# First two batches' strided attention in 32-query form, probabilities turned in place, and the second weight's columns permuted, in an attention and gated-feed-forward kernel

## The chip, the cores and the metric

The kernel runs on one core of a Trainium2 chip. The metric is the device time in microseconds (us) of one launch. The engines are named as the profile names them: PE (TensorE matmul) and PEld (its weight load), DVE (VectorE), ACT (ScalarE), POOL (GpSimd) and SP (SyncE, which issues nearly all DMAs).

## The reference

Eight batches of eight heads (576 positions, 64 wide) go through masked attention: heads 0 to 3 see the last 32 positions ("local"), heads 4 to 7 see earlier positions with the same remainder modulo 32 ("strided"). The result, 4608 rows of 512, goes through a feed-forward layer.

```python
scores = scale * np.matmul(q, k.transpose(0, 1, 3, 2))
mask_local = (rel >= 0) & (rel < stride)                     # stride = 32
mask_strided = (rel >= 0) & (pos[None, :] % stride == pos[:, None] % stride)
scores = np.where(masks[None, :, :, :], scores, -1000000000.0)
attn = np.exp(scores - np.max(scores, axis=-1, keepdims=True))
attn = attn / (np.sum(attn, axis=-1, keepdims=True) + 1e-09)
attn_out = np.matmul(attn, v).astype(np.float32)
x = attn_out.transpose(0, 2, 1, 3).reshape(B * S, H * D)
h = x @ w_in                                                 # 512 -> 2048
g = h * np.clip(h + 3.0, 0.0, 6.0) / 6.0
return g @ w_out                                             # 2048 -> 512
```

## The kernel before

**Work.** Heads go in pairs (`pair(g)`): in a batch the pairs 0 and 1 are local, 2 and 3 strided. A pair is loaded, turned so that the 64 features lie on partitions (for batch 0 by matmuls with an identity, L364; later by DVE), multiplied to scores (L593 or L601), put through the softmax on DVE, POOL and ACT, turned again, and multiplied with the values (L381, L392 or L728). The output of a pair is one 128-row piece of x, one of four along the 512 features. `keep_x` (L402) puts it away. In batches 0 and 1 each piece is split at once in a high part (ACT, L419) and the remainder (DVE, L422), since the feed-forward's matmuls take each fp32 number as two parts and multiply three times (high by high, high by low, low by high).

**Feed-forward.** Batches 0 to 2 run plainly (`ffn`, L807): L848 to L850 make a 128-column chunk of h from the four pieces of x and the first weight `wi`, ACT, DVE and POOL gate and split it, L825 to L827 multiply it with the second weight `wo`. Batches 3 and 4 run as one `super_tile` (L1165), and batches 5, 6, 7 and the last 64 rows of all batches in two `fast_tile` calls (L1263), with fewer products by Strassen's scheme. In `fast_tile` the gated values are the moving operand and pieces of the second weight the stationary one (L1441 to L1446): the 128 output columns of one product are taken with `w[:, q, h, d::2]`, every second column of 256.

**Weights.** They arrive as 8-byte numbers. `weight_part` (L258) loads 512 KB from SP, ACT makes the upper and lower bits (L281, L285), DVE joins them (L289), ACT or POOL makes the high part (L295, L297) and POOL the remainder (L301). There are 32 such loads, 16 of them issued in the first 37 us.

**Strided pairs.** With `wide` (batch 0 and batches 2 to 7) a strided pair has 32 score matmuls of 64 queries and 36 keys (L593); half of each result is of use, and four ACT copies for each head pick it (L619), after which POOL adds the mask (L633). Without it (batch 1) there are 64 matmuls of 32 queries and 18 keys (L601), and one DVE operation reads the scores and adds the mask (L626). An fp32 matmul of these kinds stands in the trace as two matmuls and two weight loads, so these are 64 and 128 in its counts. Probabilities are turned in batches 0 and 1 by DVE, block by block into the operand's tile (`turn`, L677 and L680; the very first pair by matmuls, `stand`, L364 with the name `pe`). From batch 2 on DVE turns them in place (`flip`, L683) and ACT sets the blocks out (`spread`, L690 and L693).

**Order.** The order of all instructions is set before the run by `Plan.emit` (L96): each step has an engine or a choice of engines, a cost, and a due time (`T0` is the time at which batch 0's feed-forward is wanted). A list scheduler walks through its own clock and writes the instructions in that order; each engine then runs its own stream in order, and waits at an instruction for what it needs. Where the planner sees PE idle by over 0.64 us in the first 100 us, it writes matmuls without use there (`idle`, L1550; L1560 is the first group, L1562 the later ones).

Of the kernel before, what the change touches and what calls it, by code (L numbers as in the profile page):

```python
# [29 lines left out]
TOK = 512  # L30
TURNS = ((0, 2, 1, 3), (2, 0, 3, 1)) + ((0, 2, 1, 3),) * 6
AHEAD = 27.0
OPEN = 6.0
HIENG = {"ACT": 0.63, "POOL": 0.7}

T0 = 44.0
TILE = 98.5
SUPER = 182.0  # L40
SECOND = 142.0
# [132 lines left out]
def attention_ffn(ctx: ExitStack, tc, q, k, v, w_in, w_out, out):  # L174
# [85 lines left out]
    def weight_part(k, w, g, i):  # L260
        key = wkey(w, g, i)
        fc = FQ * g if w == "i" else FQ * g + i + 1
        due = T0 + fc * TILE / NFC - 5.0 + 0.01 * k
        fkey = ("x", 1, 1 - (k // 2 % 2 if k < 20 else 0), k % 2)
        name = f"{w}{g}{i}"

        def load():
            if w == "i":
                src = w_in[i * P:(i + 1) * P, g * TOK:(g + 1) * TOK]
            else:  # L270
                src = w_out[(g * FQ + i) * P:(g * FQ + i + 1) * P, :]
            raw = new(wp, key, [P, TOK, 2], I32, f"raw{name}")
            nc.sync.dma_start(raw, src.bitcast(I32).rearrange("p (n t) -> p n t", t=2))
# [12 lines left out]

        def join():
            f = tiles[fkey]
            nc.vector.scalar_tensor_tensor(out=f, in0=f, scalar=3, in1=bits(),  # L289
                                           op0=ALU.logical_shift_left, op1=ALU.bitwise_or)  # L290

        def hi(e):
            t = new(wp, key, [P, 2, TOK], F32R, f"w{name}")
            if e == "ACT":
                nc.scalar.copy(t[:, 0], tiles[fkey].bitcast(F32))  # L295
            else:
                nc.gpsimd.tensor_copy(t[:, 0], tiles[fkey].bitcast(F32))  # L297

        def lo():
            t = tiles[key]  # L300
            nc.gpsimd.tensor_tensor(out=t[:, 1], in0=tiles[fkey].bitcast(F32), in1=t[:, 0].bitcast(F32), op=ALU.subtract)  # L301
# [21 lines left out]
    def either(us):  # L323
        return {"POOL": us, "DVE": us}

    def zero(key, pool, shape, dtype, us, due, name):

        def go(e):
            on(e).memset(new(pool, key, shape, dtype, name), 0.0)
            if key[0] == "e":  # L330
                t = tiles[key]
                on(e).memset(t[:, :NQB * WIN].rearrange("p (u x) -> p u x", x=WIN)[:, :, 2 * PAD:], 1.0e-9)
                on(e).memset(t[:, NQB * WIN:NQB * WIN + 8 * PAD].rearrange("p (u x) -> p u x", x=PAD)[:, :, NPOS:NPOS + 1], 1.0e-9)
        op(either(us), 0, go, writes=[key], due=due)

    def timing(g):
        b = g // NPAIR
# [60 lines left out]
    def x_keys(b, c):  # L398
        return [("x", b, c, i) for i in range(2)] if b < 2 else [raw_key(b, c)]

    def keep_x(nm, b, c, puts, due):

        xk, lk = x_keys(b, c), ("left", c, b)
        strided = c >= NPAIR // 2
        begun = []
        for n, (bkey, what, place, size, rest) in enumerate(puts):
            def to(i, place=place, rest=rest):
                return place(left[c][:, LEFT * b:LEFT * b + LEFT] if rest else tiles[xk[i]])

            def homes():  # L410
                if not begun:
                    begun.append(1)
                    for i, x in enumerate(xk):
                        new(xp, x, [P, TOK], F32R if b < 2 else F32, f"x{nm}{i}")

            def hi(bkey=bkey, what=what, to=to, rest=rest):
                if not rest:
                    homes()
                nc.scalar.copy(to(0), what(tiles[bkey.key]))  # L419

            def lo(bkey=bkey, what=what, to=to):
                nc.vector.tensor_tensor(out=to(1), in0=what(tiles[bkey.key]), in1=to(0).bitcast(F32), op=ALU.subtract)  # L422
# [3 lines left out]
            op("ACT", 0.15 + size * (0.0019 if strided else 0.00085), hi, reads=[bkey] + (xk if rest else []), writes=kk, give=bkey if last and whole else None, due=due + n)  # L426
            if not whole:
                op("DVE", 0.15 + size * (0.002 if strided else 0.00105), lo, reads=[bkey], writes=kk, give=bkey if last else None, due=due + 0.2 + n)

# [3 lines left out]
    def pair(g):  # L433
# [237 lines left out]
        for j in range(2):  # L671
            def turn(j=j):
                at, e = tiles[akeys[j]], e_whole(j)
                for a in range(n // PAD):
# [3 lines left out]
                        continue  # L678
                    for h in range(2):
                        nc.vector.transpose(at[PAD * (a + h):PAD * (a + h) + PAD, :, rows], e[rows, :, PAD * h:PAD * h + PAD])  # L680
            if b >= 2:
                def flip(j=j):
                    nc.vector.transpose(e_whole(j)[:, :, :2 * PAD if loc else PAD], e_whole(j)[:, :, :2 * PAD if loc else PAD])  # L683

# [13 lines left out]
                op("ACT", 6 * 0.31 if loc else 4 * 0.36, spread, reads=[ekeys[j]], writes=[akeys[j]], due=due - 1.9 + j)  # L698
# [18 lines left out]
        def values():  # L717
# [12 lines left out]
        op("PE", 1.25 * slow, values, reads=[*akeys, *vkeys], writes=[*vb, *xk, lk], take=vb, due=due - 1001,  # L730
           room=0.0 if early else ROOM, mode="v")
        if first:
            half = S // 2
# [56 lines left out]

    def out_ops(i, uk, name, rows, due, last):
        def ob():
            o = new(xp, uk, [P, DM], F32, f"ob{name}_{i}")
            if last and i % 2:
                nc.vector.tensor_scalar_mul(o, tiles["acc", i], 1.0 / 6.0)
            else:
                nc.scalar.activation(o, tiles["acc", i], AF.Copy, scale=1.0 / 6.0)

        def store():
            o = tiles[uk]  # L800
# [9 lines left out]
    def ffn(b):  # L810
        s0, puts = start[b], []
        chunk = TILE / NFC
        xk = {c: x_keys(b, c) if b < 2 else [("x", 1, c, i) for i in range(2)] for c in range(NCC)}

        def mm2(fc, gk):
            wkeys = [wkey("o", fc // FQ, fc % FQ), wkey("o", fc // FQ, fc % FQ) + ("lo",)]
# [17 lines left out]
        def first_product(fc):  # L834
# [3 lines left out]
            for n_, c in enumerate(TURNS[b]):  # L838
                wkeys = [wkey("i", fc // FQ, c), wkey("i", fc // FQ, c) + ("lo",)]

                def mm1(n_=n_, c=c, wkeys=wkeys):
# [6 lines left out]
                    nc.tensor.matmul(ph, wih, xh, start=n_ == 0, stop=False)  # L848
                    nc.tensor.matmul(ph, wih, xl, start=False, stop=False)  # L849
                    nc.tensor.matmul(ph, wil, xh, start=False, stop=n_ == NCC - 1)  # L850
                op("PE", 0.683, mm1, reads=xk[c] + wkeys, writes=[pk],
                   due=s0 + (fc + n_ * 0.12) * chunk, mode="f")
            return fc, pk, uk, gk

# [430 lines left out]
    def fast_tile(si):  # L1285
# [87 lines left out]
        def second_of(s):  # L1373
# [5 lines left out]
            for j, nm in enumerate(SECONDS):  # L1379
# [53 lines left out]
                for d in range(2):  # L1433
                    bank = ("acc", d + 2 * (nm in ("P2", "P5", "P3")))

                    def mm(d=d, bank=bank, gks=gks, wk=wk, fresh=fresh, nm=nm):
# [3 lines left out]
                        w = home(wk).rearrange("p q (h d) -> p q h d", h=2)  # L1440
                        for q in range(2):  # L1441
                            gh, gl = (half_of(gks[q], x) for x in range(2))
                            wh, wl = (w[:, q, h, d::2] for h in range(2))
                            nc.tensor.matmul(acc, wh, gh, start=fresh and q == 0, stop=False, skip_group_check=not fresh)  # L1444
                            nc.tensor.matmul(acc, wh, gl, start=False, stop=False, skip_group_check=not fresh)  # L1445
                            nc.tensor.matmul(acc, wl, gh, start=False, stop=q == 1, skip_group_check=not fresh)  # L1446
# [62 lines left out]
    def first_tiles():  # L1509
        tiles["qplain"] = ap.tile([P, S + STRIDE * PAD], F32, tag="qq", name="qplain")  # L1510
        tiles["kplain"] = ap.tile([P, PAD + 2 * S], F32, tag="kk", name="kplain")
        nc.gpsimd.memset(tiles["kplain"][:, :PAD], 0.0)
        nc.gpsimd.memset(tiles["qplain"][:, S:].rearrange("c (r m) -> c r m", m=PAD)[:, :, NPOS:], 0.0)
        tiles["at64"] = ap.tile([P, 2, 3 * QB], F32, tag="vt", name="at64")
    op("POOL", 0.1, first_tiles, writes=["plain", ("at64", 0), ("at64", 1)], due=-30)
# [80 lines left out]
```

## Time and profile before

| what | before |
|---|---|
| runs, us | 873.19, 875.98, 877.65; median 875.98 |
| profiled execution: its time, its span | 873.75 us, 871.9 us |
| PE busy | 851.9 us (98%) |
| PEld, DVE, ACT, POOL busy | 687.7, 539.3, 557.8, 614.7 us |
| first matmul of the feed-forward (L848) | 38.96 us after the span's start |
| mean granted TensorE clock | 0.992 |
| moved by DMA | 179.12 MB, mean 205 GB/s |

The profiled time is 1.85 us longer than the span. Busy shares are means over the whole span: PE is busy nearly always, so a change matters where PE waits or where its matmuls take longer than they must. A row of the timeline gives the start, the length, the engine, the line and operation, the tiles, the shape and how many instructions were merged, and in brackets how long the engine sat idle before, and who ended that; "issue" stands for a wait for which the profile shows nobody. A row of the windows gives for each engine the busy time and, as (x...), the instructions in that stretch, then the granted TensorE clock as a share of the full one, the busy share of the 16 DMA engines, and GB/s.

### The profile page before, as it was taken

What the parts mean: (1) busy time and instruction counts of PE and PEld (TensorE: products, weight loads), DVE (VectorE), ACT (ScalarE), POOL (GpSimd) and SP (SyncE); (2) the same over time, 40 slices, a digit from 0 to 9 for tenths busy, and PEclk for the clock granted to TensorE, in tenths of its full rate; (3) what the DMA queues carried; (4) which work ended last, traced back from release to release, by engine and by line L of the source; (5) the groups of instructions that cost most, each with busy time, mean ns of one, the idle gap of its engine ahead of it and who ended that gap; (6) DMA issues with size and microseconds to landing.
All of it is one profiled execution on the core that took longest, in us unless ns stands there. A gap on an engine that the chain in (4) does not pass through costs nothing.

```text
span 871.9 us, 18946 instructions
## 1 busy us (share of the span) xinstructions
PE 851.9 (98%) x6962; PEld 687.7 (79%) x6962; DVE 539.3 (62%) x898; ACT 557.8 (64%) x1246; POOL 614.7 (70%) x606
## 2 busy tenths in 40 slices
PE   9889999999999999999999999999999999999996
PEld 6667778878878788888888888788888778888884
DVE  5698877344544548454546672566776987655586
ACT  3697657678778766777668855776645555454441
POOL 4688876688447799756767993666974978667572
PEclk9899999999999999999999999999999999999998
DMA  8968714888974456899999998976566577766536
GB/s 214 322 140 243 220 28 93 236 265 239 299 200 111 112 141 163 233 250 259 259 262 282 300 284 213 253 188 198 181 195 183 178 207 214 231 190 188 178 121 145
DMA packets 323308, 179.12 MB, mean 205 GB/s; under 512 B 182864, under 2 KB 300368, under 8 KB 323216
## 3 DMA queue, kind: packets, MB, share of 16 engines
q1 hardware_dynamic: 318564, 176.27, 71.9%
q10 hardware_dynamic: 4652, 1.64, 0.9%
q8 instruction: 55, 0.90, 0.4%
q14 instruction: 37, 0.30, 0.1%
HBM read 136.97 MB, written 40.89 MB: 204 GB/s over the span
## 4 chain that ended last, share of the span: by engine, by line
PE 87%; DMA 5%; POOL 3%; DVE 2%; issue 1%; ACT 1%; SPq 0%; ACTq 0%; POOLq 0%
PE P L1121 9%; PE P L1123 8%; PE P L1122 8%; PE cP L1444 6%; PE cP L1446 6%; PE cP L1445 6%; PE acc L825 5%; PE ph L848 5%; PE acc L827 5%; PE acc L826 4%; PE ph L850 4%; PE ph L849 4%; PE acc L1206 4%; PE acc L1208 3%; PE acc L1207 3%; PE pv L392 2%
## 5 line engine op out<-in xcount | busy, mean ns | idle before, releaser
L1462 DVE SCALAR_TENSOR_TENSOR C<-cP,C 128x512 f32<-128x512 f32 x96 | 65.7, 688 | 44.9 <-PE cP L1446 44.3
L787 POOL TENSOR_TENSOR gl<-u,gh 128x512 fp32r<-128x512 f32 x48 | 65.2, 1359 | 32.2 <-ACT gh L783 16.0
L1133 DVE TENSOR_TENSOR G<-P,G 128x512 f32<-128x512 f32 x64 | 44.0, 689 | 65.6 <-PE P L1123 52.8
L1121 PE MATMUL P<-B_T,wr 128*128 128x512 f32 x192 | 76.2, 397 | 3.4 <-ACT G L1128 2.3
L825 PE MATMUL acc<-wo,gh 128*128 128x512 f32 x192 | 77.2, 402 | 0.0
L827 PE MATMUL acc<-wo,gl 128*128 128x512 f32 x192 | 75.2, 392 | 0.1
L1123 PE MATMUL P<-B_T,wr 128*128 128x512 f32 x192 | 75.0, 391 | 0.0
L1122 PE MATMUL P<-B_T,wr 128*128 128x512 f32 x192 | 74.9, 390 | 0.0
L826 PE MATMUL acc<-wo,gh 128*128 128x512 f32 x192 | 74.9, 390 | 0.0
L1128 ACT COPY G<-P 128x512 f32<-128x512 f32 x64 | 37.6, 587 | 54.1 <-PE P L1123 53.8
L1359 POOL TENSOR_TENSOR sp<-G,sp 128x512 fp32r<-128x512 f32 x34 | 47.2, 1399 | 25.6 <-ACT sp L1355 23.4
L658 POOL TENSOR_TENSOR e<-e,st 128x144 f32<-128x144 f32 (+1 forms) x64 | 44.6, 700 | 20.2 <-DVE st L654 17.2
L772 DVE SCALAR_TENSOR_TENSOR u<-u,ph 128x512 f32<-128x512 f32 x48 | 32.7, 684 | 37.9 <-ACT u L769 37.8
L848 PE MATMUL ph<-x,wi 128*128 128x512 f32 x128 | 51.9, 406 | 2.0 <-DVE u L772 1.1
L693 ACT COPY atloc<-e 32x192 f32<-32x192 f32 x144 | 50.8, 353 | 2.5 <-DVE e L683 1.1
L849 PE MATMUL ph<-x,wi 128*128 128x512 f32 x128 | 50.1, 391 | 1.1 <-DVE fo L289 0.7
L769 ACT ACTIVATE u<-ph,three 128x512 f32<-128x512 f32 x48 | 33.0, 688 | 27.7 <-PE ph L850 27.3
L850 PE MATMUL ph<-x,wi 128*128 128x512 f32 x128 | 50.2, 392 | 0.5 <-POOL wi L301 0.5
L1121 PE MATMUL P<-B_B,wr 128*128 128x512 f32 x120 | 47.1, 393 | 0.0
L637 DVE TENSOR_REDUCE st<-e 128x8 f32<-128x144 f32 (+1 forms) x64 | 25.6, 413 | 34.5 <-POOL e L633 34.3
L1123 PE MATMUL P<-B_B,wr 128*128 128x512 f32 x120 | 46.8, 390 | 0.0
L1122 PE MATMUL P<-B_B,wr 128*128 128x512 f32 x120 | 46.8, 390 | 0.0
(604 smaller groups left out, 2669.1 us busy)
## 6 DMA issues: line engine op xcount, KB each, us to landing
wr<-dA SPq DMA_DIRECT2D x72, 256.0 KB
or<-do SPq DMA_DIRECT2D x32, 512.0 KB
wr<-dSu SPq DMA_DIRECT2D x48, 256.0 KB
wr<-dSv SPq DMA_DIRECT2D x48, 256.0 KB
or<-do SPq DMA_DIRECT2D x48, 256.0 KB
rawi<-in_moe_w_in_dram SPq DMA_DIRECT2D x16, 512.0 KB
rawo<-in_moe_w_out_dram SPq DMA_DIRECT2D x16, 512.0 KB
do<-wo SPq DMA_DIRECT2D x16, 512.0 KB
```

Source lines behind the costliest of these rows:

```text
L787: (nc.vector if tail else nc.gpsimd).tensor_tensor(out=to, in0=src(), in1=tiles[gk[0]].bitcast(F32), op=ALU.subtract)
L825: nc.tensor.matmul(acc, gh, woh, start=fc == 0, stop=False)
L826: nc.tensor.matmul(acc, gh, wol, start=False, stop=False)
L827: nc.tensor.matmul(acc, gl, woh, start=False, stop=end)
L848: nc.tensor.matmul(ph, wih, xh, start=n_ == 0, stop=False)
L849: nc.tensor.matmul(ph, wih, xl, start=False, stop=False)
L850: nc.tensor.matmul(ph, wil, xh, start=False, stop=n_ == NCC - 1)
L1121: nc.tensor.matmul(ph, wh, xh, start=fresh and k == 0, stop=False, skip_group_check=not fresh)
L1122: nc.tensor.matmul(ph, wh, xl, start=False, stop=False, skip_group_check=not fresh)
L1123: nc.tensor.matmul(ph, wl, xh, start=False, stop=k == 1, skip_group_check=not fresh)
L1444: nc.tensor.matmul(acc, wh, gh, start=fresh and q == 0, stop=False, skip_group_check=not fresh)
L1462: nc.vector.scalar_tensor_tensor(out=tiles[ck], in0=tiles[bank], scalar=1.0 / 6.0, in1=tiles[ck], op0=ALU.mult, op1=ALU.add)
```

## The change

1. `wide` now holds from batch 2 on, so batch 0's two strided pairs take the form that batch 1's have: twice as many score matmuls, no ACT copies, no mask on POOL.
2. Batch 1's pairs and batch 0's strided pairs are turned in place on DVE; the blocks are then set out one by one, each on ACT, POOL or DVE, whichever the planner finds free (`FREE = 2`). POOL resets a column of the strided tiles after that, as from batch 2 on.
3. In batches 0 and 1 the parts of a piece of x have keys of their own, so that high and low parts of the two halves need not follow each other (`xh`, `xl`).
4. The columns of `wo` are stored with the even ones of each half of 256 ahead of the odd ones, by a strided read in the three steps that make its two parts. `fast_tile` then takes 128 adjacent columns, and `out_ops` puts the order right by a strided write.
5. `T0` is 43.0 in place of 44.0; a remainder copy of x is due 3 later (`LEFTS`).

```diff
-T0 = 44.0
+T0 = 43.0
...
         def lo():
-            t = tiles[key]
-            nc.gpsimd.tensor_tensor(out=t[:, 1], in0=tiles[fkey].bitcast(F32), in1=t[:, 0].bitcast(F32), op=ALU.subtract)
+            nc.gpsimd.tensor_tensor(out=part(1), in0=whole(), in1=part(0).bitcast(F32), op=ALU.subtract)
...
-            kk = [lk] if rest else xk
...
+            kk = [lk] if rest else xk if whole else [("xh", b, c, n)] + ([] if n else xk)
...
-        wide = not loc and b != 1
+        wide = not loc and b > 1
...
-            if b >= 2:
+            if b >= 2 or b == 1 or b == 0 and not loc:
...
+                if b < FREE:
+                    for a in range(n // PAD):
+                        for h in range(1 + loc):
...
+                            op({"ACT": 0.33, "POOL": 0.42, "DVE": 0.37} if loc else {"ACT": 0.4, "POOL": 0.5, "DVE": 0.44}, 0, set_out,
+                               reads=[ekeys[j], ("zero",) + akeys[j]], writes=own, due=due - 1.9 + j)
...
+            o = new(xp, uk, [P, DM], F32, f"ob{name}_{i}").rearrange("p (h e d) -> p h d e", h=2, d=2)
+            acc = tiles["acc", i].rearrange("p (h d e) -> p h d e", h=2, d=2)
...
-                            wh, wl = (w[:, q, h, d::2] for h in range(2))
+                            wh, wl = (w[:, q, h, P * d:P * d + P] for h in range(2))
```

The planner writes a new order. On PE, between the scores of batch 0's last pair (`ps_30`, `ps_31`) and the second feed-forward chunk, before has this (`pe` turns the probabilities of pair 1, `ph` is the feed-forward's first product, `x_00` and `x_01` the parts of the first piece of x):

```order
L593 MATMUL ps_31_739<-kt_3_289,qt_3_288 64x36
L1562 MATMUL idle<-ident 128x384 x3
L364 MATMUL pe_10_801<-ident,e_130 64x96 x6
L848 MATMUL ph_0_814<-x_00_702,wi_790 128x512
L849 MATMUL ph_0_814<-x_01_703,wi_790 128x512
L850 MATMUL ph_0_814<-x_00_702,wi_790 128x512
```

And the changed kernel has this:

```order
L610 MATMUL ps_31_756<-kt_3_290,qt_3_289 32x18
L1590 MATMUL idle<-ident 128x384
L875 MATMUL ph_0_844<-x_00_746,wi_822 128x512
L876 MATMUL ph_0_844<-x_01_747,wi_822 128x512
L877 MATMUL ph_0_844<-x_00_746,wi_822 128x512
```

The scores ahead of it are twice as many rows (32 in place of 16 for each of the two heads), as are those of pair 2 earlier. Five rows of `idle` ahead of the first feed-forward product are gone (10 are left of 15), and `pe_10`, which stood ahead of it, now stands six products later, together with `pe_11`. The values of pair 3 (`pv_30`) have moved ahead of the products with the second piece of x.

On ACT, the order around the copy of pair 1's turned probabilities (`at<-pe_10`) is in before (`fi` and `rawi` are a weight's upper and lower bits, `e` a tile of scores, `x` and `left` parts of x):

```order
L619 COPY e_228<-ps_31_739 32x8x18 x4
L419 CAST x_20_774<-pv_21_710 128x4x4x16
L713 COPY at_195<-pe_10_801 128x288
L281 ACTIVATE fi_828<-rawi_359 128x512
L295 CAST wi_840<-fi_727 128x512
```

In the changed kernel:

```order
L654 ACTIVATE e_130<-e_130 128x8x18
L738 COPY at_196<-pe_10_861 128x288
L738 COPY at_196<-pe_11_877 128x288
L283 ACTIVATE fi_900<-rawi_360 128x512
L654 ACTIVATE e_229<-e_229 128x8x18
L287 ACTIVATE rawi_360<-rawi_360 128x512
L305 CAST wi_948<-fi_858 128x512
```

The copies of scores are gone, both copies of pair 1's probabilities stand together, and the bits of the fourth weight part (`rawi_360`) and all later ones still stand behind them.

SP's stream is the same through its first 70 rows, past all 32 weight loads.

More of the change, by code (lines that the diff above doesn't have):

```diff
@@ L32 @@
 AHEAD = 27.0
+LEFTS = 3.0
+FREE = 2
 OPEN = 6.0
 HIENG = {"ACT": 0.63, "POOL": 0.7}
-T0 = 44.0
+T0 = 43.0
 TILE = 98.5
@@ L290, in join, with whole, part @@
                                            op0=ALU.logical_shift_left, op1=ALU.bitwise_or)
+        def whole():
+            f = tiles[fkey].bitcast(F32)
+            return f if w == "i" else f.rearrange("p (h e d) -> p h d e", h=2, d=2)
+        def part(x):
+            t = tiles[key][:, x]
+            return t if w == "i" else t.rearrange("p (h d e) -> p h d e", h=2, d=2)
         def hi(e):
-            t = new(wp, key, [P, 2, TOK], F32R, f"w{name}")
+            new(wp, key, [P, 2, TOK], F32R, f"w{name}")
             if e == "ACT":
-                nc.scalar.copy(t[:, 0], tiles[fkey].bitcast(F32))
+                nc.scalar.copy(part(0), whole())
             else:
-                nc.gpsimd.tensor_copy(t[:, 0], tiles[fkey].bitcast(F32))
+                nc.gpsimd.tensor_copy(part(0), whole())
         def lo():
-            t = tiles[key]
-            nc.gpsimd.tensor_tensor(out=t[:, 1], in0=tiles[fkey].bitcast(F32), in1=t[:, 0].bitcast(F32), op=ALU.subtract)
+            nc.gpsimd.tensor_tensor(out=part(1), in0=whole(), in1=part(0).bitcast(F32), op=ALU.subtract)
         op("SP", 0.53, load, writes=[key], due=-49 + 0.01 * k if k < 4 else -48.4 + 0.01 * k if k < 6 else -2 + 0.1 * k if k < 16 else due - 20.0, early=7.0 if k < 16 else due - 30.0, after=1.6 if k < 16 else 1.25)
@@ L422, in lo @@
                 nc.vector.tensor_tensor(out=to(1), in0=what(tiles[bkey.key]), in1=to(0).bitcast(F32), op=ALU.subtract)
-            kk = [lk] if rest else xk
             last = all(x[0] is not bkey for x in puts[n + 1:])
             whole = rest or b >= 2
-            op("ACT", 0.15 + size * (0.0019 if strided else 0.00085), hi, reads=[bkey] + (xk if rest else []), writes=kk, give=bkey if last and whole else None, due=due + n)
+            kk = [lk] if rest else xk if whole else [("xh", b, c, n)] + ([] if n else xk)
+            op("ACT", 0.15 + size * (0.0019 if strided else 0.00085), hi, reads=[bkey] + (xk if n or rest else []), writes=kk, give=bkey if last and whole else None, due=due + n + LEFTS * rest)
             if not whole:
-                op("DVE", 0.15 + size * (0.002 if strided else 0.00105), lo, reads=[bkey], writes=kk, give=bkey if last else None, due=due + 0.2 + n)
+                op("DVE", 0.15 + size * (0.002 if strided else 0.00105), lo, reads=[bkey, ("xh", b, c, n)], writes=[("xl", b, c, n)], give=bkey if last else None, due=due + 0.2 + n)
     def pair(g):
@@ L697, in pair, with set_out @@
                 op("DVE", 0.55 if loc else 0.4, flip, writes=[ekeys[j]], due=due - 2 + j)
-                op("ACT", 6 * 0.31 if loc else 4 * 0.36, spread, reads=[ekeys[j]], writes=[akeys[j]], due=due - 1.9 + j)
+                if b < FREE:
+                    for a in range(n // PAD):
+                        for h in range(1 + loc):
+                            def set_out(e, a=a, h=h, j=j):
+                                rows = slice(PAD * a, PAD * a + PAD)
+                                x, at = e_whole(j)[rows], tiles[akeys[j]]
+                                x = x[:, :, PAD * h:PAD * h + PAD] if loc else x
+                                at = at[PAD * (a + h):PAD * (a + h) + PAD, :, rows]
+                                if e == "ACT":
+                                    nc.scalar.copy(at, x)
+                                else:
+                                    on(e).tensor_copy(at, x)
+                            own = [(akeys[j], 2 * a + h)] if a + h else akeys[j:j + 1]
+                            op({"ACT": 0.33, "POOL": 0.42, "DVE": 0.37} if loc else {"ACT": 0.4, "POOL": 0.5, "DVE": 0.44}, 0, set_out,
+                               reads=[ekeys[j], ("zero",) + akeys[j]], writes=own, due=due - 1.9 + j)
+                else:
+                    op("ACT", 6 * 0.31 if loc else 4 * 0.36, spread, reads=[ekeys[j]], writes=[akeys[j]], due=due - 1.9 + j)
                 if not loc:
@@ L729, in values @@
                                      ats[j][:, i].rearrange("p (a m) -> p a m", a=4)[:, :, :NPOS], start=True, stop=True)
-        op("PE", 1.25 * slow, values, reads=[*akeys, *vkeys], writes=[*vb, *xk, lk], take=vb, due=due - 1001,
+        op("PE", 1.25 * slow, values, reads=[*akeys, *vkeys] + [(x, i) for x in akeys for i in range(8) if b < FREE], writes=[*vb, *xk, lk], take=vb, due=due - 1001,
            room=0.0 if early else ROOM, mode="v")
@@ L813, in ffn @@
         xk = {c: x_keys(b, c) if b < 2 else [("x", 1, c, i) for i in range(2)] for c in range(NCC)}
+        parts = {c: [(x, b, c, n) for x in ("xh", "xl") for n in range(3)] if b < 2 else [] for c in range(NCC)}
         def mm2(fc, gk):
@@ L850, in mm1 @@
                     nc.tensor.matmul(ph, wil, xh, start=False, stop=n_ == NCC - 1)
-                op("PE", 0.683, mm1, reads=xk[c] + wkeys, writes=[pk],
+                op("PE", 0.683, mm1, reads=xk[c] + parts[c] + wkeys, writes=[pk],
                    due=s0 + (fc + n_ * 0.12) * chunk, mode="f")
@@ L1512, in first_tiles @@
         nc.gpsimd.memset(tiles["kplain"][:, :PAD], 0.0)
+        nc.gpsimd.memset(tiles["qplain"][:, 2 * S:2 * S + SPARE], 0.0)
         nc.gpsimd.memset(tiles["qplain"][:, S:].rearrange("c (r m) -> c r m", m=PAD)[:, :, NPOS:], 0.0)
```

7 lines of the change are left out of this document (3 added, 4 removed).

## The prediction

> **What bounds the kernel now.** I read the page first, then PE's timeline, windows cut along it, and PE's waits.
>
> ```profile
> PE 851.9 (98%) x6962; PEld 687.7 (79%) x6962; DVE 539.3 (62%) x898; ACT 557.8 (64%) x1246; POOL 614.7 (70%) x606
> q8 instruction: 55, 0.90, 0.4%
> ```
>
> PE is the bound; only the time before its stream runs steadily, its stalls, and the pace of its matmuls can be changed. The stalls are in the early part:
>
> ```profile
> 18.11 1.02 PE L593 MATMUL ps<-kplain,qplain 64*64 64x36 f32 x55 [0.80 <-issue]
> ...
> 22.10 0.58 PE L364 MATMUL pe<-ident,e 96*64 96x96 f32 x5
> 25.05 1.43 PE L364 MATMUL pe<-ident,e 96*64 96x96 f32 x19 [2.37 <-issue]
> ...
> 38.96 0.50 PE L848 MATMUL ph<-x,wi 128*128 128x512 f32 x1
> ...
> 43.01 1.25 PE L381 MATMUL pv<-at,v 64*64 64x32 f32 x72
> 44.19 0.50 PE L848 MATMUL ph<-x,wi 128*128 128x512 f32 x1
> 45.36 0.40 PE L849 MATMUL ph<-x,wi 128*128 128x512 f32 x1 [0.68 <-DVE fo L289]
> ```
>
> The first two stalls fall inside a group of equal matmuls, wait for nobody ("issue"), and the third is put down to a DVE step that has no part in this product. A count shows what they share. These windows are cut at the stalls and at the first feed-forward matmul:
>
> ```profile
> 0.00:18.10 18.10, 15.94 (x349) 12.04 (x349) 10.32 (x27) 5.60 (x9) 7.69 (x27) 1.00 0.85 189
> 18.10:25.04 6.94, 4.57 (x126) 3.80 (x127) 4.23 (x13) 3.42 (x11) 3.66 (x7) 1.00 1.00 329
> 25.04:38.95 13.91, 13.90 (x283) 10.43 (x282) 9.62 (x25) 9.41 (x25) 6.99 (x8) 0.75 0.88 291
> 38.95:45.35 6.40, 5.73 (x98) 4.28 (x98) 4.33 (x10) 5.37 (x14) 5.93 (x9) 1.00 1.02 416
> ```
>
> From stall to stall PE ran 126 matmuls, then 283 + 98 = 381, three times 127. The page's queue of instructions moved 0.90 MB in 55 packets for 6962 matmuls and as many weight loads: 127 matmuls to a packet. So I read these stalls as PE waiting for the next packet of its own program; the packet ends lie at matmul 349, 475, 602, 729 and 855. [...]
>
> A packet is late because it stands in the DMA engines behind the data already asked for. PE enters one packet and asks for the next; that comes about when data issued at the same moment lands. From the chain of waits (start, length; issue to landing):
>
> ```profile
> 28.79 6.62 DMA rawo<-in_moe_w_out_dram
> 35.43 10.20 DMA rawo<-in_moe_w_out_dram
> ```
>
> PE entered packets at 18.11 and 25.05, 6.9 us apart, about as long as the first of these took. From 25.05 to 45.36 three packets were passed; data issued at 35.43 landed at 45.63, 0.3 us after PE resumed. Here matmuls were many and small, so a packet lasts PE 1 to 3 us; later, with 0.23 us each (six take 1.36, below), it lasts 29 us.
>
> **The change part by part.**
>
> *Scores.* Batch 0's two strided pairs go from 64 to 128 matmuls each. The time itself is little: 1.02 us of the 55 above is 1.2 for 64; batch 1's form is
>
> ```profile
> 62.91 1.27 PE L601 MATMUL ps<-kplain,qplain 64*32 64x18 f32 x128
> ```
>
> so 0 to 0.2 us. But ahead of the first feed-forward matmul stand 349 + 126 + 283 = 758 matmuls, and now 758 + 128 for the scores, less 10 for five rows of `idle` (two matmuls each), less 12 for `pe_10`: 864. Before, that product lay 97 short of the packet that begins after 855; now it lies behind it. So the feed-forward, which began at 38.96, now begins when that packet has come.
>
> *When it comes.* Up to 25.05 nothing that sets a packet's time has changed: SP's loads are the same. Next come 127 matmuls that include kp_3, both `pe`, and part of ps_1, 4 us at full clock and up to 6 at half, so PE enters packet 602 at 29.1 (as before) to 31.5. I take 30.5. The two chain rows give landings of 35.41 and 45.63 for issues 6.64 us apart, so each us of issue costs 1.54: asked for at 30.5, packet 729 is there at 35.41 + 1.71 x 1.54 = 38.0. By then SP has issued all twelve loads of this stretch:
>
> ```profile
> 32.78 4.19 SPq L273 DMA_DIRECT2D rawo<-in_moe_w_out_dram  x4
> 38.30 7.61 SPq L350 DMA_DIRECT2D qn<-in_q_dram  x4
> ```
>
> The last of them, issued at 36.97 at the latest, lands by the same slope at 45.63 + 1.54 x 1.54 = 48.0. Packet 855 thus comes between 45.36 (as before) and 48.0, or 49 behind the small `qn` pieces; I take 47.5: **+2.1 us**.
>
> *What PE still has to do then.* Before, at 45.36, PE had done 13 products (3.0 us at 0.23), `pe_10` and `pe_11`, and 72 matmuls `pv`. Now these lie ahead, with one `idle`:
>
> ```profile
> 35.97 2.20 PE L1562 MATMUL idle<-ident 128*128 128x384 f32 x6
> 38.10 0.93 PE L364 MATMUL pe<-ident,e 96*64 96x96 f32 x12
> ```
>
> That is 3.0 + 2 x 0.86 (38.96 less 38.10) + 1.18 (44.19 less 43.01) + 2.13 / 3 = **+6.6 us**.
>
> *Clock.* PE stood from 22.6 to 25.04, and then ran at half the clock:
>
> ```profile
> 22.60:25.04 2.44, 0.08 (x1) 0.00 (x0) 1.44 (x6) 0.32 (x1) 1.85 (x4) 1.00 1.12 317
> 26.00:32.00 6.00, 6.00 (x151) 4.83 (x150) 4.38 (x14) 4.37 (x10) 1.25 (x2) 0.50 0.74 220
> ```
>
> Half clock was there 3.4 us after the idling began, and held to 32 at least. Now packet 729 (from 38.0) is used up in some 2 us and PE stands from 40 to 47.5. If half clock lasts to 50.5 it takes 1.5 us of products; if the long wait stretches it to 54, 3.3; if it is over by 47.5, nothing. **+2.2**.
>
> *Parts side by side, softmax steps moved, blocks set out.* They shorten the way to x: four ACT copies and POOL's mask go for each of batch 0's strided heads, DVE turns once in place of four times, and the blocks go to whichever of ACT, POOL and DVE is free. PE never waits for these engines before 51 us, so nothing is gained there. What this can give PE are its later stalls:
>
> ```profile
> 53.06 0.49 PE L848 MATMUL ph<-x,wi 128*128 128x512 f32 x1 [0.92 <-ACT x L419]
> 53.96 0.50 PE L849 MATMUL ph<-x,wi 128*128 128x512 f32 x1 [0.41 <-DVE x L422]
> ...
> 57.66 0.50 PE L850 MATMUL ph<-x,wi 128*128 128x512 f32 x1 [0.45 <-POOL wi L301]
> ```
>
> ```profile
> PE ph L848 <- DVE u L772: 1.1, 2, 0.8
> ```
>
> These are 1.78 + 1.1 us, some 0.2 us more each with the restart: 0 to 3.8. Against it stands that ACT's copy of `pe_10` waits for PE, and the fourth weight part and all later ones are queued behind it; DVE joins and POOL splits them, and PE waits for those. I take **-2.2**.
>
> *Columns of the second weight.* A strided load of weights takes 194 ns, an adjacent one 188:
>
> ```profile
> L1122 PEld LDWEIGHTS P<-B_T,wr 128*128 128x128 f32 x192 | 36.1, 188 | 7.5
> ...
> L1444 PEld LDWEIGHTS cP<-sp,or 128*128 128x128 f32 x88 | 17.1, 194 | 3.7 <-DVE C L1462 0.2
> ```
>
> ```profile
> 595.65 0.39 PE L1121 MATMUL P<-B_T,wr 128*128 128x512 f32 x1
> ...
> 597.01 0.39 PE L1444 MATMUL cP<-sp,or 128*128 128x512 f32 x1
> ...
> 598.41 0.39 PE L1121 MATMUL P<-B_T,wr 128*128 128x512 f32 x1
> ```
>
> Six P matmuls took 1.36 us from start to start, six cP 1.40. The pace differs by 7 ns here, and the loads by 6; two `fast_tile` calls have 2 x 4 x 7 x 2 x 2 x 3 = 672 such matmuls. I take 4.8 ns, since a start is given to 10 ns only and a load may hide in part: **-3.2**, bounds 0 and -4.5. [...]
>
> *Strided reads and writes it brings.* The three steps that split `wo` and the 20 copies of results read or write with a stride of 8 bytes, beside PE. ACT's upper-bit step already reads so. For POOL no row shows it; the remainder now takes
>
> ```profile
> L301 POOL TENSOR_TENSOR wo<-fo,wo 128x512 fp32r<-128x512 f32 x16 | 21.3, 1338 | 0.7 <-ACT wo L295 0.4
> ```
>
> and half as long again would be 0.7 us for each of 16, 11 us in all, at worst all of it PE's. It reads one of two operands so; I take 0.
>
> Sum: 2.1 + 6.6 + 2.2 - 2.2 - 3.2 = **+5.5 us**. From the profiled 873.75 that is 879.25; the median of the runs is 2.2 higher, so I forecast 881.5.
>
> **The rivals.**
>
> *The packet comes when it came before.* At 45.36, with PE at full clock, all later stalls gone and the columns as computed: 6.6 - 3.8 - 3.2 = -0.4, no difference that a measurement of this kernel can tell (about 0.5%, 4.4 us). For it: packets 602 and 729 came at the same distance behind their requests whatever PE did. Against: 602 is entered later, as its matmuls are more. Chance 0.17.
>
> *The stalls are not the program's packets.* Then PE starts at 38.96 or up to 1 us earlier (fewer `idle`), the three stalls ahead of it stay, and it gains 2.2 to 3.8 and 3.2: -5.4 to -8, about 869. The count of 126 and 381 speaks against it. [...] Chance 0.12.
>
> *The columns bring nothing.* +8.7, 884.7: chance 0.12. *POOL's strided reads delay the second weight*, deciding once L301 takes well over 1.34 us where PE waits for it: with half of the 11 us on PE's path, 887. Chance 0.05.
>
> **How the numbers follow.** The forecast's own case has 0.54 and runs from +2 to +9; 0.41 of it lies above +4.4. With the last two rivals slower gets 0.58; within 0.5% 0.28 (the other 0.13 and most of the first rival's 0.17); faster 0.14. The range leaves out the second rival and the far end of the last: 874.5 (-1.5) to 888 (+12).
>
> **What would show it.** The first product (line 875) starts at 45 to 49; there is an "issue" wait, or one with an odd name, just ahead of it, at matmul 855 from the start; another from about 19.6 to 25. The granted clock is half for some us around 48. Weight loads of cP read 188 ns. If the first product starts at or before 39, the reading of the packets is wrong; if cP stays at 194, the columns are.

## The result and the profile after

The changed kernel takes 884.25 us (median of 6 runs, 882.90 to 886.12), the kernel before beside it 875.63 (6 runs): a ratio of 1.0109, 95% interval 1.0093 to 1.0125. It is slower, by 8.1 to 10.9 us. The forecast was 881.5. The profiled execution took 886.12 us with a span of 883.9, so the profiled pair lies 12.4 us apart, some 4 more than the medians; its differences are read with that in mind.

The page of the changed kernel, busy time and queue of instructions:

```profile
PE 851.6 (96%) x7080; PEld 687.9 (78%) x7080; DVE 541.7 (61%) x879; ACT 559.9 (63%) x1246; POOL 622.6 (70%) x630
q8 instruction: 56, 0.92, 0.4%
```

PE is busy as long as before (851.6 and 851.9 us), with 118 matmuls more; the span grew by 12.0 us, so on balance it grew by waiting (within the busy time, by the estimates below, the matmuls at half clock, some 4.8 us, and the faster ones with the second weight, 4.4 us, about offset each other). PE's timeline has the waits:

```profile
18.21 1.19 PE L610 MATMUL ps<-kplain,qplain 64*32 64x18 f32 x119 [1.35 <-issue]
25.05 1.71 PE L373 MATMUL qp<-ident,qn 72*64 72x72 f32 x24 [5.26 <-issue]
39.81 0.62 PE L753 MATMUL pv<-atstr,v 128*64 128x72 f32 x5 [1.66 <-issue]
46.28 0.30 PE L610 MATMUL ps<-kt,qt 64*32 64x18 f32 x5 [4.51 <-issue]
46.51 1.65 PE L1590 MATMUL idle<-ident 128*128 128x384 f32 x2
47.38 1.20 PE L875 MATMUL ph<-x,wi 128*128 128x512 f32 x1
50.65 2.29 PE L373 MATMUL pe<-ident,e 96*64 96x96 f32 x24
57.46 0.31 PE L753 MATMUL pv<-atstr,v 128*64 128x72 f32 x2 [1.76 <-ACT atstr L716]
58.82 1.67 PE L753 MATMUL pv<-atstr,v 128*64 128x72 f32 x30 [1.05 <-ACT atstr L716]
60.42 0.80 PE L875 MATMUL ph<-x,wi 128*128 128x512 f32 x1
```

The four rows that wait on "issue" are the first instructions of new packets: counted through the trace (a matmul and its weight load are two instructions, PE's own wait for a semaphore is one more), PE resumes at instructions 705, 961, 1473 and 1729, which differ by multiples of 256. In before, counted the same way, the waits that end at 18.11, 25.05 and 45.36 stand at 705, 961 and 1729, although the profile puts the last down to DVE. The last wait ends at 46.28, and the first feed-forward product follows at 47.38; it was at 38.96. The row at 50.65 is `pe_10` and `pe_11`. Behind them is a wait that before did not have: `pv_30` waits twice for blocks that ACT sets out.

The clock, in windows of 2 us (the columns as before, the granted clock third from the end):

```profile
22.00:24.00 2.00, 0.00 (x0) 0.00 (x0) 0.00 (x0) 0.00 (x0) 0.43 (x2) 0.50 0.99 352
44.00:46.00 2.00, 0.00 (x0) 0.00 (x0) 0.00 (x0) 0.00 (x0) 0.00 (x0) 0.50 1.00 401
50.00:52.00 2.00, 2.00 (x17) 1.36 (x17) 0.48 (x1) 0.00 (x0) 2.00 (x3) 0.50 0.37 58
52.00:54.00 2.00, 2.00 (x19) 1.71 (x16) 0.00 (x0) 1.42 (x4) 0.38 (x1) 0.87 0.81 163
60.00:62.00 2.00, 2.00 (x12) 1.57 (x9) 1.61 (x3) 1.65 (x4) 2.00 (x2) 0.50 0.00 0
```

The clock is at half (0.50) from 22 to beyond 52 us, and again around 60, after PE has stood 2.81 us for `pv_30`. While PE stands at 44, no engine works, and the DMA engines are busy all the time (a share of 1.00).

What ACT does at that second place (its timeline):

```profile
48.94 0.31 ACT L654 ACTIVATE e<-e 128x144 f32<-128x144 f32 x1
52.29 0.40 ACT L738 COPY at<-pe 128x288 f32<-128x288 f32 x1 [3.03 <-PE pe L373]
...
56.16 0.40 ACT L716 COPY atstr<-e 32x256 f32<-32x256 f32 x1
56.96 0.40 ACT L716 COPY atstr<-e 32x256 f32<-32x256 f32 x1
58.32 0.40 ACT L716 COPY atstr<-e 32x256 f32<-32x256 f32 x1
```

ACT stands 3.03 us before the copy of `pe_10`, and the blocks of `pv_30` are queued behind it. The two rows that price the steps with the second weight:

```profile
L1472 PEld LDWEIGHTS cP<-sp,or 128*128 128x128 f32 x88 | 16.5, 188 | 3.5
L310 POOL TENSOR_TENSOR wo<-fo,wo 128x512 fp32r<-128x512 f32 x16 | 21.3, 1339 | 2.2 <-ACT wo L305 1.6
```

The loads of the second weight take 188 ns in place of 194, and POOL's strided remainder 1339 ns in place of 1338.

### The profile page after: what moved, and what is told of

It reads as the page before. It is cut to its first block, busy times and chain, and to the rows that moved or that the text cites. A ratio compares the mean times of both kernels' runs of the same rounds, so it can differ in the third digit from the quotient of the medians.

```text
span 883.9 us, 19220 instructions
## 1 busy us (share of the span) xinstructions
PE 851.6 (96%) x7080; PEld 687.9 (78%) x7080; DVE 541.7 (61%) x879; ACT 559.9 (63%) x1246; POOL 622.6 (70%) x630
## 4 chain that ended last, share of the span: by engine, by line
PE 80%; POOL 6%; DVE 4%; issue 4%; ACT 3%; DMA 2%; SPq 0%; POOLq 0%; DVEq 0%; ACTq 0%
PE P L1148 7%; PE P L1150 7%; PE P L1149 7%; PE ph L875 5%; PE acc L852 5%; PE cP L1471 5%; PE cP L1473 5%; PE cP L1472 5%; PE ph L877 5%; PE ph L876 5%; PE acc L854 4%; PE acc L853 4%; PE acc L1233 2%; PE ps L610 2%; PE acc L1234 2%
## 5 line engine op out<-in xcount | busy, mean ns | idle before, releaser
L1160 DVE TENSOR_TENSOR G<-P,G 128x512 f32<-128x512 f32 x64 | 43.9, 688 | 50.5 <-PE P L1150 40.0
L667 POOL TENSOR_TENSOR e<-e,st 96x384 f32<-96x384 f32 (+1 forms) x64 | 43.6, 683 | 41.2 <-DVE st L663 36.8
L660 DVE TENSOR_REDUCE st<-e 96x6 f32<-96x390 f32 (+1 forms) x64 | 27.3, 426 | 49.4 <-ACT e L654 31.8
L875 PE MATMUL ph<-x,wi 128*128 128x512 f32 x128 | 53.2, 415 | 1.8 <-DVE u L797 1.8
L877 PE MATMUL ph<-x,wi 128*128 128x512 f32 x128 | 51.0, 398 | 0.7 <-POOL wi L310 0.7
L876 PE MATMUL ph<-x,wi 128*128 128x512 f32 x128 | 50.9, 398 | 0.0
```

## The experiments

The theory: PE's early time is set by the packets of its own program; the 32-query scores put so many instructions ahead of the first product that it falls behind one packet more, which comes late because it stands behind data. The chief rival: the new order (blocks set out one by one, ACT held up behind `pe_10`) delays PE, and the waits on "issue" are something else. Each ratio is to the kernel before on the same chip, whose medians were 874.43 to 875.34 us; "first product" is the first feed-forward matmul of the profiled execution.

### Parts of the change undone or done alone

**64-query scores given back to the changed kernel.**

```diff
-        wide = not loc and b > 1
+        wide = not loc and b != 1
```

> The changed kernel with batch 0's strided pairs given back their 64-query scores (parts side by side, turns in place, set-outs and the columns stay). The first feed-forward product is then matmul 742 from the start, ahead of the packet end at 855 and behind the one at 729. Theory (PE waits for packets of its own program): the first product starts at 37 to 40 us in place of 47.4, no stall of over 2 us stands ahead of it after 30 us, and the time is 866 to 872 us, before less the columns' 3 to 4 and less some later stalls. First rival (the delay comes from the new order: blocks set out by ACT behind pair 1's copies): the time stays at 880 to 886. Second rival (the columns bring nothing in the end): 873 to 877.

877.05 us, ratio 1.0021 (1.0002 to 1.0041). PE's timeline and its chain of waits:

```profile
35.16 0.50 PE L875 MATMUL ph<-x,wi 128*128 128x512 f32 x1
```

```profile
PE ph L875 <- DVE u L797: 5.9, 5, 1.5
PE pv L753 <- POOL atstr L718: 3.3, 2, 2.7
```

(This kernel is called the first run below.) The first product comes 12 us sooner, sooner even than expected, so the scores alone move it, as the theory has it. They cost 0.9% (1.0109 against 1.0021), 7.7 us, on top of the rest. But the time is not 866 to 872: what is left of the change costs too, against the columns alone (below), and PE now waits for DVE's gating and POOL's blocks. The traces show where: at its hundredth product of 512 columns this kernel is 2.1 us ahead of the columns alone (72.51 against 74.57 us), at its two hundredth 4.0 behind (105.46 against 101.44), and three of the waits for DVE's gating, 3.3 us together, lie between. So the changed kernel, 12.1 us behind this one at the hundredth product, is 6.7 behind at the two hundredth. Neither pure theory stands.

**32-query scores alone in the kernel before.**

```diff
-        wide = not loc and b != 1
+        wide = not loc and b > 1
...
```

The changed kernel's one clearing step for the tile of queries (POOL, at the start) goes with it.

> The kernel before with one part of the change alone: batch 0's strided pairs in the 32-query form. The first product becomes matmul 896, behind the packet end at 855, and all else (set-outs, parts, columns) is as before. Theory: the first product starts at 45 to 49 us in place of 38.96 and the time is 883 to 890, 8 to 14 us over before. First rival (new order and set-outs are the cause): the time of before within 2 us, 874 to 878, and the first product at 38 to 41. A third way, that the matmuls' own time is the cost (64 more of each kind at some 18 ns): 1 to 2 us over before, with no new stall.

897.51 us, ratio 1.0275 (1.0243 to 1.0308): the right sign, but twice what was expected, and the first product, at 51.33, comes later than the 45 to 49 expected.

```profile
45.72 0.33 PE L601 MATMUL ps<-kt,qt 64*32 64x18 f32 x11 [4.23 <-issue]
45.98 2.93 PE L1563 MATMUL idle<-ident 128*128 128x384 f32 x4
51.33 0.80 PE L848 MATMUL ph<-x,wi 128*128 128x512 f32 x1
...
125.03 0.39 PE L827 MATMUL acc<-wo,gl 128*128 128x512 f32 x1 [1.96 <-issue]
...
150.91 0.80 PE L848 MATMUL ph<-x,wi 128*128 128x512 f32 x1 [2.62 <-DVE u L772]
```

The packet comes at 45.72, as in the changed kernel; then matmuls without use, at half the clock (2.93 us for four, where before has 2.20 for six), and `pe_10` still stand ahead of the product. A hundred products of 512 columns are begun by 84.31 us here, by 84.64 in the changed kernel, by 72.10 in before: the scores alone make the whole delay of the early part, 12.2 us. The rest, some 11 of 23.1 by the medians, comes after 85 us, from later waits of which the last two rows show some (1.96 us on "issue", and 2.62 for DVE). So the rest of the change makes the narrow scores cheaper after 85 us; by which of its steps was not tried.

**The columns alone in the kernel before.** The diff is item 4 of the change.

> The kernel before with the permuted columns of the second weight alone; its order of instructions is otherwise that of before. By the forecast's term: weight loads of cP fall from 194 to 188 ns, six cP matmuls from 1.40 to 1.37 us, and the time is 3 to 4.5 us under before, about 872. Rival (the stride of 8 bytes costs PE nothing): the time of before, 875 to 876. If the strided reads in the split of wo delay POOL where PE waits for it, 877 or more, and the remainder's step takes well over 1.34 us.

871.22 us, ratio 0.9963 (0.9946 to 0.9981).

```profile
L1452 PEld LDWEIGHTS cP<-sp,or 128*128 128x128 f32 x88 | 16.5, 188 | 3.5
```

```profile
596.61 0.40 PE L1452 MATMUL cP<-sp,or 128*128 128x512 f32 x1
...
597.99 0.39 PE L1129 MATMUL P<-B_T,wr 128*128 128x512 f32 x1
```

3.2 us less (1.7 to 4.7 by the interval), as forecast. Six cP matmuls take 1.38 us here, but that is one stretch, read to 10 ns. Over all neighbouring cP matmuls of the two traces (589 pairs each), one starts 233.6 ns after the other in before and 227.1 here, while the P products stay at 228.2 and 227.3: 6.5 ns for each of 672 are 4.4 us. So the strided read costs PE its pace here although it is of neighbours but one: 194 against 188 ns a load, and the interval of the ratio leaves out 1.

**Set-outs without DVE**, in the kernel of the first run:

```diff
-op({"ACT": 0.33, "POOL": 0.42, "DVE": 0.37} if loc else {"ACT": 0.4, "POOL": 0.5, "DVE": 0.44}, 0, set_out,
+op({"ACT": 0.33, "POOL": 0.42} if loc else {"ACT": 0.4, "POOL": 0.5}, 0, set_out,
```

> The kernel of the first run (64-query scores given back) with the set-outs of blocks on ACT and POOL alone, none on DVE. That kernel took 877.05 us where the columns alone took 871.22, so the parts, turns and set-outs cost 5.8 us there; its PE waited 5.9 us for DVE's gating step u, behind groups of three set-outs of 0.65 us each on DVE, for which the planner counts 0.37 to 0.44. If these are the cost: PE's waits for u fall to 1 to 2 us and the time to 870 to 873. Rival (the other parts of the new order cost it, or ACT and POOL become late in DVE's place): 875 to 879.

880.05 us, ratio 1.0054 (1.0033 to 1.0074): not better than the first run (the two intervals just overlap), so this guess fell. PE's waits for `u` did go (5.9 to 1.2 us), but others came in their place, of which the longest is

```profile
PE acc L854 <- POOL gl L812: 2.1, 2, 1.9
```

**The old due times**, in the kernel of the first run (`T0` 44, no delay for remainder copies).

> The kernel of the first run (64-query scores given back, 877.05 us) with the old due times, T0 44 and no delay for remainder copies. The columns alone took 871.22. If the shifted due times cost those 5.8 us: 870 to 873. If the blocks set out one by one and the parts side by side cost them, by the order that the planner makes of them: 875 to 879.

881.51 us, ratio 1.0071 (1.0054 to 1.0088). The due times are not the cost; they save some 4 us.

**Turns block by block as before**, in the kernel of the first run; with `FREE` 0, too, no block is set out one by one.

```diff
-            if b >= 2 or b == 1 or b == 0 and not loc:
+            if b >= 2:
```

> The kernel of the first run (64-query scores given back, 877.05 us) with the probabilities of the first two batches turned block by block by DVE as before, so that no block is set out one by one; the parts side by side, the due times and the columns stay. The columns alone took 871.22. If the turns in place and the set-outs cost the 5.8 us: 870 to 873. If the parts side by side or the due times, by the order that follows from them, cost them: 875 to 879.

880.84 us, ratio 1.0076 (1.0051 to 1.0101). So the turns in place and the set-outs are not the cost either; they too save some 5 us. Here PE waits for POOL:

```profile
PE ph L877 <- POOL wi L310: 3.9, 5, 1.5
PE ph L875 <- DVE u L797: 2.6, 1, 2.6
PE ph L875 <- POOL wi L307: 2.1, 2, 1.5
```

With 64-query scores and the columns, every kernel that has the parts side by side (these three and the first run) is 5 to 10 us slower than the columns alone. That leaves the parts, by the order that the planner makes with them, as the suspect, unless two of the others cost it only together; they were not tried alone, and the cause stays open there.

### Instructions and packets

**The 46 small idle matmuls at the start replaced by two large ones**, in the changed kernel.

```diff
-            for i in range(FEW):
-                nc.tensor.matmul(warm[0][PAD * (i % 4):PAD * (i % 4) + PAD, :PAD], tiles["ident",][:, :PAD], tiles["ident",][:, :PAD],
+            for i in range(2):
+                nc.tensor.matmul(warm[0][:, :3 * P], tiles["ident",], tiles["ident",].unsqueeze(1).to_broadcast([P, 3, P]), start=True, stop=True)
```

> The changed kernel with the 46 small idle matmuls at the start (184 instructions with their weight loads) replaced by two large ones of about the same length (8 instructions). Nothing else moves, but every packet end comes 88 matmuls later in the work, so that the first product (now matmul 776) stands ahead of the packet end at 855. Theory: the first product starts at 38 to 41 us in place of 47.4, and the time is 868 to 877, 7 to 15 us under the changed kernel. Rival (order and set-outs): the first product stays at 46 to 48 and the time at 882 to 886. Rival (PE's early matmuls and idles keep the clock up, the stalls do not matter): the same or slower, 884 to 888.

883.94 us, ratio 1.0116 (1.0094 to 1.0138): no change. The theory missed.

```profile
18.81 0.39 PE L373 MATMUL qp<-ident,qn 96*64 96x96 f32 x4 [2.77 <-issue]
25.37 0.45 PE L610 MATMUL ps<-kplain,qplain 64*32 64x18 f32 x31 [2.39 <-issue]
...
45.38 0.68 PE L610 MATMUL ps<-kt,qt 64*32 64x18 f32 x45 [2.59 <-issue]
46.86 1.20 PE L875 MATMUL ph<-x,wi 128*128 128x512 f32 x1
```

The waits still end at instructions that lie multiples of 256 apart, now at other matmuls, and a new one stands at 18.81 (instruction 449). By the trace's records of queue q8 the first packet was fetched at 15.76 us, at 8.56 in the changed kernel. The small idles run when PE has nothing else to do (1.36 to 2.85 us), and with them the packet is fetched 7.2 us sooner; without them PE has fewer instructions to read and as many fewer in hand. So it is not the number of the packet that counts, as my expectation had it, but, as I read these times, how many instructions must be read while the data flows fast (in the changed kernel 391 GB/s from 20 to 22 us, 172 from 8 to 10).

**Large idles in the kernel before replaced by eight small ones each**, after the first group.

```diff
-        nc.tensor.matmul(warm[0][:, :3 * P], tiles["ident",], tiles["ident",].unsqueeze(1).to_broadcast([P, 3, P]), start=True, stop=True)
...
+        for i in range(8):
+            nc.tensor.matmul(warm[0][PAD * (i % 4):PAD * (i % 4) + PAD, :PAD], tiles["ident",][:, :PAD], tiles["ident",][:, :PAD],
+                             start=True, stop=True)
```

> The kernel before, where each large idle matmul after the first group (two matmuls and two weight loads, 0.37 to 0.44 us) becomes eight small ones (32 instructions, about 0.27 us). PE's useful work and its order stay; PE has some 410 more instructions ahead of the first feed-forward product and a little less time to spend on them. Theory (PE waits for packets of 256 instructions): two packet ends more lie ahead of that product (it is instruction 1927 in place of 1517), so it starts at 45 to 49 us in place of 38.96, behind stalls that wait for nobody, and the time is 879 to 886, 5 to 11 us over before. Rival (order of the work and the length of matmuls): the first product at 38 to 39.5 and the time of before within 1.5 us, 873 to 876.

882.09 us, ratio 1.0072 (1.0046 to 1.0098), within the theory's range and outside the rival's.

```profile
32.04 0.54 PE L381 MATMUL pv<-at,v 64*64 64x32 f32 x20 [1.92 <-issue]
...
39.01 1.29 PE L593 MATMUL ps<-kt,qt 64*64 64x36 f32 x37 [2.13 <-issue]
...
43.04 0.80 PE L848 MATMUL ph<-x,wi 128*128 128x512 f32 x1
```

Useful work, its order and its engines are those of before; only the number of PE's instructions grew (by 392 ahead of the first product), and it costs 6 us, though the single runs spread widely (873.02 to 885.76). The first product is at 43.04, sooner than expected, since the packets came sooner too: PE went on at instructions 1473 and 1729 at 32.04 and 39.01 us, at 35.61 and 45.36 in before.

**No large idles in the changed kernel.** The matmul moves under the condition that holds for the first group alone, so one of the ten stays.

```diff
         if warm[0] is None:
...
-        nc.tensor.matmul(warm[0][:, :3 * P], tiles["ident",], tiles["ident",].unsqueeze(1).to_broadcast([P, 3, P]), start=True, stop=True)
+            nc.tensor.matmul(warm[0][:, :3 * P], tiles["ident",], tiles["ident",].unsqueeze(1).to_broadcast([P, 3, P]), start=True, stop=True)
```

> The changed kernel without its large idle matmuls (the first group's small ones stay): 40 instructions fewer ahead of the first product, which moves from behind the packet end at instruction 1729 to 20 instructions ahead of it. The useful work and its order stay. Theory: the first product starts at 41 to 43 us in place of 47.4, some ten products run, and then PE stands until 46 to 47 as before; the time is 878 to 882, 2 to 6 us under the changed kernel. Rival (order and set-outs): the first product and the time stay, 882.5 to 885.5. Rival (the idles keep the clock up): slower, 886 to 890.

878.11 us, ratio 1.0043 (1.0028 to 1.0059): 0.66% or 5.8 us under the changed kernel.

```profile
35.65 1.23 PE L610 MATMUL ps<-kt,qt 64*32 64x18 f32 x117 [2.97 <-issue]
36.80 0.80 PE L875 MATMUL ph<-x,wi 128*128 128x512 f32 x1
...
41.72 1.21 PE L373 MATMUL pe<-ident,e 96*64 96x96 f32 x20 [1.38 <-issue]
```

The first product now lies ahead of the packet end at instruction 1729, and it moved by 10.6 us, more than expected: both packets came over 4 us sooner (35.65 for 39.81, 41.72 for 46.28). The idles, planned for time in which the planner saw PE idle, cost twice here: their own time (1.65 us for each of the last two, at half clock; 0.91 for one at full clock, at 14.62), and 36 instructions (the expectation counted 40). This run alone does not part the two; the clock did not make it slower.

**Light loads in the changed kernel.**

```diff
+            if 4 <= k < 16:
+                n = TOK // 4
+                nc.sync.dma_start(tiles[key][:, :n], src[:, :n].bitcast(I32).rearrange("p (n t) -> p n t", t=2))
+                return
             raw = new(wp, key, [P, TOK, 2], I32, f"raw{name}")
...
```

Three quarters of the columns of these twelve weights are left out; twelve steps on DVE and POOL that set them to zero come in.

> The changed kernel with twelve of the first sixteen weight loads (those issued from 28.7 to 38 us) cut to a quarter of their columns; the rest of each tile is set to zero at the start, so the product with these weights leaves out three quarters of their columns. PE's stream is the same. If packets are late because they stand behind data in the DMA engines: those asked for at 33.3 and 37.4 come 2 to 4 us after the request in place of 4.1 and 6.5, the first product starts at 41 to 44 in place of 47.4, and the time is 876 to 881. If they take their time whatever else is asked for: first product at 46 to 48, time 882.5 to 886. If PE waits for x or the weights and not for its program, the first product would also be at 46 to 48, as x does not hang on these loads.

877.37 us, ratio 1.0029 (1.0011 to 1.0047): 0.8% or 7.0 us under the changed kernel.

```profile
36.53 0.40 PE L763 MATMUL pv<-atstr,v 128*64 128x72 f32 x5 [0.82 <-issue]
40.26 0.30 PE L620 MATMUL ps<-kt,qt 64*32 64x18 f32 x5 [2.18 <-issue]
...
41.36 1.20 PE L885 MATMUL ph<-x,wi 128*128 128x512 f32 x1
```

**Light loads in the kernel before**, the control, with the same edit.

> The kernel before with the same twelve weight loads cut to a quarter (three quarters of those weights' columns are left out, set to zero at the start), the control to the changed kernel with light loads, which went from 884 to 877.4. If light loads help there because PE's packets come sooner, little is to be had here: one packet stall of 1.1 us at 44.3 and 0 to 1 us of half clock, so 873 to 875.5. If light loads help for another reason (weights and queries sooner, an emptier memory), the gain is about as large as there, 6 to 7 us: 868 to 869.

874.99 us, ratio 1.0005 (0.9991 to 1.0019): nothing. Its first product starts at 38.71:

```profile
38.71 0.50 PE L858 MATMUL ph<-x,wi 128*128 128x512 f32 x1
```

The two together decide between the packets and the rivals that were named. PE's stream is that of the kernel it is compared with, and x does not hang on these loads; with less data in the queues, the kernel that waits for packets gained 7 us, and the one that hardly waits for them gained none. The trace's records of queue q8 show why. For the two packets ahead of the first product, the time from PE's entering the packet before to the start of the fetch, in us:

| kernel | packet 729 | packet 855 |
|---|---|---|
| before | 4.1 | 7.4 |
| changed | 3.9 | 4.0 |
| before, light loads | 1.9 | 0.8 |
| changed, light loads | 1.1 | 1.3 |

**Columns alone, no large idles.**

> The kernel before with the permuted columns (871.22 us in its own run) and without the large idle matmuls. Taking the idles from the changed kernel brought its first product from 47.4 to 36.8 us and its time from 884 to 878. Here no packet end lies between the idles and the first product, and that product started at 38.1 with one idle ahead of it; what is late next is the second piece of x (waits at 52 to 55 us). Theory: the first product 0.5 to 2 us earlier, the packet at instruction 1729 asked for a little earlier, and 868 to 871 us. Rival (the idles only fill time in which PE waits for x or weights anyway): the time of the columns alone, 870.5 to 872. Rival (the idles keep the clock up): 873 to 876.

870.50 us, ratio 0.9953 (0.9936 to 0.9970), beside 0.9963 for the columns alone: the two cannot be told apart, and either is faster than both kernels. Here the idles' instructions carry no packet end across the first product (it stays just behind the packet end at 1473), and they cost little or nothing.

## Why the prediction was right, and where it was not

*The packets: right.* The first product was to start at 45 to 49, behind an "issue" wait at matmul 855; it starts at 47.38, behind a wait of 4.51 us at instruction 1729. More instructions with the same work make before slower (1.0072), and less data in the queues brings the packets sooner (their fetches begin 1.1 and 1.3 us after PE enters the packet before, in place of 3.9 and 4.0). The rival that the stalls are not the program's packets has fallen. The rival that packet 855 comes when it came before is near by the time of the packet (0.9 us), but not by its sum: it had the full clock and all later stalls gone, and neither held. With the large idles in the small ones' place, PE stood at instruction 449 until 18.81 us, 3.05 us after the fetch of its first packet had begun (15.76), so by this trace it had nothing in hand there beyond the 448 instructions it had passed.

*When packet 855 comes: near, in part by luck.* 46.28 against 47.5, a delay of 0.9 us in place of 2.1. The way there was off twice, in opposite directions. At half the clock PE entered packet 602 at 33.4 us (instruction 1217), not at 30.5, so that 729 came at 39.81 and not at 38.0; and 855 came 6.5 us after that, where the forecast gave it 9.5.

*The clock: under-sized.* The half clock held to 52.5 us and came back from 59.4 to 62.8, where the forecast had it end at 50.5. By these rows it cost some 4.8 us after 46.28 in place of 2.2 (an estimate: half of 6.2 and of 3.4 us). The row at 50.65 is 2.29 us for the 24 matmuls that the forecast put at 1.72.

*Later stalls, -2.2: wrong, and of the wrong sign.* This is the step that failed. The forecast named the danger (what is queued on ACT behind the copy of `pe_10`), but let the gain win. In the changed kernel PE waits 2.8 us for `pv_30`'s blocks there. The waits for x (0.92 and 0.41) did go, but those for `wi` and for `u` grew from 0.5 and 1.1 to 0.7 and 1.8. And with the scores given back, what is left of the change without the columns costs 0.58% (1.0021 against 0.9963), about 5.1 us; by which of its parts stays open.

*Columns, -3.2: right.* 3.2 by the run that has them alone (1.7 to 4.7 by its interval). By the pace in the traces they give 4.4, so the 4.8 ns were on the low side. The measured time lies nearest the rival in which they bring nothing (884.7), but that is the other terms' doing.

*Strided reads on POOL, 0: right, or nearly.* The remainder takes 1339 against 1338 ns in the changed kernel; with the columns alone it took 1360, some 0.4 us for all 16.

Taken apart by the runs, in this order, the change is columns -3.2, parts, turns and set-outs +5.1, scores +7.7: 9.6 us. The forecast had -3.2, -2.2 and (2.1 + 6.6 + 2.2) = +10.9: two errors of 7.3 and 3.2 that partly cancel, and leave 5.5 for 9.6. That the total came this near is in part luck. The last two terms of the runs are sure to some 2 us each, and the parts do not simply add up. The scores alone cost 2.75%; in the changed kernel they delay the hundredth product by 12.1 us, more than the +10.9, but the time at the end shows only a part of it.

## What to carry to other kernels

Where an engine waits for nobody the profile shows, count its instructions from wait to wait. Here the counts were multiples of 256, and it was the program itself that was late; what helped was fewer instructions while the DMA engines were busy (5.8 us less without the large idles, their own time included), or less data asked for then (7.0 us less). The form with twice as many small matmuls cost no busy time here (851.6 us against 851.9) and still moved the first product behind one more packet, from 38.96 to 47.38 us. Where parts of a change meet through a planner's order, price each alone and in company: here the same scores cost 0.9% in one order and 2.75% in the other.

## What the runs showed of the hardware

Instructions read in idle time were not lost here: 46 small matmuls at 1.4 to 2.9 us let the next packet be fetched at 8.56 us and not at 15.76. From the start of a packet's fetch to PE's going on it took 2.3 to 2.5 us at instruction 1729 (43.04 to 45.36 before, 43.83 to 46.28 in the changed kernel), and 2.4 to 3.0 at the other waits of the two kernels.

DVE copies of blocks, for which the planner counts 0.44 us, took 0.93 us each in this place (timeline of DVE, first run; 0.63 on the mean of its eleven), and the gating that PE waits for stands behind them:

```profile
74.64 2.78 DVE L718 COPY atstr<-e 32x256 f32<-32x256 f32 x3
77.46 0.69 DVE L797 SCALAR_TENSOR_TENSOR u<-u,ph 128x512 f32<-128x512 f32 x1
```

ACT's copies of results, written with a stride of 8 bytes since the change, take 637 ns (631 with the columns alone); they took 596:

```profile
L823 ACT ACTIVATE ob<-acc 128x512 f32<-128x512 f32 x12 | 7.1, 637 | 2.4 <-PE acc L854 2.3
```
